# Single heads on quadrants of TensorE in an mLSTM followed by a rational feed-forward, with a work list derived anew

## The chip, the cores and the metric

One core of one Trainium2 chip runs the whole kernel. The metric is the device time of one execution, in microseconds; the kernel before takes 531.24 us, the median of three runs (530.92 to 532.42).

## What is computed

The reference has two stages. The first is a recurrent attention (mLSTM) over 4 batches of 8 heads, 768 steps, heads of 40 values:

```
for t in range(768):
    m_new = max(f[t] + m, i[t])
    fs, is_ = exp(f[t] + m - m_new), exp(i[t] - m_new)
    C = fs * C + is_ * outer(v[t], k[t])          # 40 x 40 per head
    n = fs * n + is_ * k[t]
    y[t] = sigmoid(o[t]) * (C @ q[t]) / max(abs(n . q[t]), 1)
```

The second takes the 3072 rows of 320 values through two matrices with a rational function between them:

```
h = x @ w_in                                      # 320 -> 2048
g = (a0 + a1 h + a2 h^2 + a3 h^3) / (1 + |b0||h| + |b1| h^2 + 1e-6)
out = g @ w_out                                   # 2048 -> 320
```

## The kernel before

**Attention.** The 768 steps are cut into chunks of 64 (`L`), and two chunks of one batch, 128 steps for all 8 heads, make a *unit*; there are 24 units, `u` = 0 to 23 (`attention`, line 841). Two units of neighbouring batches make a *pair*, `m` = 0 to 11 (`outputs`, line 1056). Heads go in twos: `NP` = 4 pairs of heads, the even head `j` = 0 on partitions 0 to 39 and the odd head `j` = 1 on partitions 64 to 103 of a tile of `DP` = 104 partitions. A unit's steps, each a piece of one engine's work, are: `lk`, `lq`, `lv`, `lf`, `la` (loads); `kp` (POOL scales the keys); `sc` (DVE's scan makes the decays `e`); `tk` and `ek` (PE transposes keys, ACT copies them to `kT`); `tq` and `eq` (PE transposes queries, ACT copies them to `qb`); `qa` (DVE, queries times decay, tile `qA`); `S` (PE, scores, tile `ps`); `P` (DVE, scores times decay, into tile `pm`); `ke` (POOL, decayed keys, the other part of `pm`); `ow` (PE, state products of the two chunks); `d0`, `u0`, `d1`, `u1` (POOL decays a state into `tm0` or `tm1`, DVE adds the product: states `sm` after the first chunk, `st` after the second). A pair's steps are `it` (PE, scores times values into two banks `y0` and `y1`), `i1` (PE adds queries times states to both banks), `ab`, `rc`, `g`, `x` (normalise and gate into `xn`), `xt`, `xh`, `xl` (transpose and split for the second stage, tile `xk`).

Two heads share one matmul by zeros in the operand: `qb` is cleared once in `_prologue` and `eq` writes the even head's queries into one half of its columns and the odd head's into the other half, with two copies of 40 partitions (lines 943 to 945). `S` (line 951) then makes 8 matmuls for a unit, each with 104 partitions, 64 columns of weights and 128 columns of queries. The states have the same form: `st` and `sm` hold 2 x 41 columns per pair of heads, with zeros where the two heads do not meet, so `decay` (line 987) works on 104 x 328 values, `update` (line 994) is two instructions of 40 partitions, and `inter` (line 1078) makes its matmuls with 104 partitions and 82 columns. Each bank `y{k}` holds heads 4k to 4k+3. `ow` reads only the decayed keys in `pm`, so it waits for `ke` and not for `P`. An f32 matmul stands in the trace as two instructions (two passes).

**Feed-forward.** Blocks of 256 rows (`n` = 0 to 11), eight tiles `i` of 256 of the 2048 columns each, make 96 tiles. A tile's steps are `f1` (PE, 16 single-pass matmuls of 256 columns, tile `ph`), `ha`, `p1`, `u`, `y`, `r0` (ACT), `p3`, `gh`, `m`, `gl` (DVE), `w`, `rm` (POOL), `f2` and `f3` (PE, 12 matmuls, tile `po`). The last tile of all is done in halves (names with `half`).

**Order.** Nothing is scheduled on the chip: `ORDER` (from line 145) is one written list of all steps, and `_Plan.listed` and `issue` emit them in that order, each engine following its own part of it strictly (`_Queue`). Six PSUM banks (`BANKS`, line 142) form one ring from which every `ph`, `ps`, `kq`, `ow`, `y` and `px` is taken; two hold `po`. Steps `hot` are 90 idle matmuls that fill PE during the start, `hz` another 24 at the end.

Of the kernel before, what the change touches and what calls it, by code (L numbers as in the profile page):

```python
# [141 lines left out]
BANKS = 6  # L142
# [15 lines left out]
sc_1 raw_i1 o0_o3 ogl_1 tq_1 raw_i2 eq_1 s1_j0 hot.65 gate.10 ow_0 pa_1 pc_1 pa_2 ke_1 o2_o3 zero.6 s0_o0.1 o2_o5
s3_j0 S_1 squares pc_2 qa_1 P_1 u0_0 ow_1 s2_o0 d1_0 hot.66 lk_3 raw_i5 lq_2 s1_o0.1 u0_1 hot.67 s0_o0 o0_j0 o2_j0
hot.68 hot.69 hot.70 hot.71 hot.72 hot.73 hot.74 hot.75 hot.76 s2_i1 s0_i1 u1_0 og_0 s3_o0.1 s1_o0 s1_i1 d1_1 raw_j1  # L160
s3_o0 it_0 i1_0 hot.77 hot.78 hot.79 ab_0 o0_o0 u1_1 s3_i1 pf_2 gate.11 sc_2 kp_2 tk_2 o2_j0.1 hot.80 s0_i2 it_0.1
rc_0 g_0 i1_0.1 ek_2 s2_i2 raw_o2 gate.12 s1_i2 ab_0.1 s0_i5 rc_0.1 gate.18 hot.81 x_0 hot.82 s3_i2 tq_2 hot.83
zero.9 ke_2 s1_i5 lv_2 hot.84 g_0.1 x_0.1 hot.85 gate zero.7 o0_i1 eq_2 hot.86 hot.87 pa_3 lq_3 oc_j0 raw_o4 lk_4
qa_2 o2_i1 s0_j1 s1_j1 xt_0 hot.88 xt_0.1 s2_i5 hot.89 pc_3 s3_i5 o2_o0 xh_0 s2_j1 o0_i2 xl_0 kp_3 s3_j1 ow_2 o0_i5
o2_i5 S_2 gate.1 tk_3 s0_o2.1 s0_o2 gate.13 u0_2 s1_o2 s2_o2 xh_0.1 s1_o2.1 d1_2 raw_o6 s3_o2 gate.14 raw_i7 u1_2
s3_o2.1 ek_3 xl_0.1 tq_3 o2_i2 o0_j1 s0_o4.1 eq_3 s0_o4 s2_o4 pf_3 P_2 f1_0_0 f1_0_0.1 o2_j1 gate.15 sc_3 gate.16
lv_3 lf_4 s1_o4.1 ke_3 kp_4 S_3 oc_j1 gate.19 s1_o4 s3_o4.1 s3_o4 ha_0_0 p1_0_0 s0_i7 f1_0_1 p3_0_0 P_3 u_0_0 lq_4
s1_i7 gate.17 o2_j1.1 s2_i7 o0_o4 ow_3 f1_0_1.1 s3_i7 w_0_0 s0_o6 o2_o4 y_0_0 ha_0_1 o0_i7 f1_0_2 f1_0_2.1 r0_0_0
lk_5 u0_3 gate.20 ogl_2 d1_3 qa_3 o2_i7 f1_0_3 gh_0_0 m_0_0 s1_o6 u_0_1 ha_0_2 w_0_1 p1_0_1 f2_0_0 f1_0_3.1 f2_0_0.1
# [6 lines left out]
u_0_5 m_0_4 o0_o6 rm_0_3 rm_0_4 ha_0_6 gl_0_3 qa_4 f3_0_3 xt_1.1 xh_1.1 w_0_5 f3_0_3.1 gate.25 gl_0_4 ow_4 S_4 u_0_6
p3_0_5 xl_1.1 zero.10 o2_o6 u0_4 P_4 p1_0_6 y_0_5 f2_0_4 r0_0_5 w_0_6 f1_1_0 d1_4 gh_0_5 m_0_5 f2_0_4.1 f3_0_4 tk_5
rm_0_5 ha_0_7 u_0_7 p3_0_6 w_0_7 ek_5 p1_0_7 u1_4 sc_5 f3_0_4.1 f1_1_0.1 y_0_6 ha_1_0 r0_0_6 gl_0_5 p3_0_7 gh_0_6
tq_5 f2_0_5 eq_5 f1_1_1 f1_1_1.1 f2_0_5.1 p1_1_0 qa_5 u_1_0 ke_5 d0_5 lk_6 gate.28 lq_6 lq_7 la_7 S_5 m_0_6 y_0_7
ha_1_1 r0_0_7 P_5 ow_5 f3_0_5 f3_0_5.1 p3_1_0 w_1_0 y_1_0 gh_0_7 m_0_7 f1_1_2 rm_0_6 rm_0_7 f2_0_6 ogl_8 gate.29  # L180
ogl_6 lf_6 gl_0_6 u_1_1 u0_5 w_1_1 f1_1_2.1 d1_5 p1_1_1 r0_1_0 gl_0_7 f2_0_6.1 f3_0_6 f3_0_6.1 f2_0_7 f2_0_7.1
gh_1_0 m_1_0 p3_1_1 f3_0_7 ha_1_2 p1_1_2 u1_5 p3_1_2 f3_0_7.1 it_2 i1_2 it_2.1 i1_2.1 lv_6 ev_0_7 u_1_2 ev_0_7.1
kp_6 y_1_1 ab_2 rc_2 sc_6 tk_6 rm_1_0 d0_6 g_2 r0_1_1 w_1_2 ke_6 f2_1_0 f2_1_0.1 lk_7 ab_2.1 ek_6 gh_1_1 gl_1_0
y_1_2 r0_1_2 x_2 m_1_1 rc_2.1 f1_1_3 f1_1_3.1 gate.26 tq_6 ha_1_3 p1_1_3 rm_1_1 gh_1_2 m_1_2 g_2.1 rm_1_2 f3_1_0
eq_6 gl_1_1 p3_1_3 u_1_3 f1_1_4 f1_1_4.1 ha_1_4 u_1_4 w_1_3 lv_7 x_2.1 qa_6 f3_1_0.1 f2_1_1 f2_1_1.1 gl_1_2 kp_7 S_6
ow_6 P_6 u0_6 p1_1_4 w_1_4 f3_1_1 p3_1_4 lf_7 lf_8 y_1_3 r0_1_3 f3_1_1.1 y_1_4 d1_6 gh_1_3 m_1_3 u1_6 f2_1_2 r0_1_4
xt_2 f1_1_5 f1_1_5.1 ha_1_5 f2_1_2.1 tk_7 ek_7 f3_1_2 f3_1_2.1 f2_1_3 f2_1_3.1 xh_2 u_1_5 d0_7 p1_1_5 xt_2.1 tq_7
gh_1_4 m_1_4 eq_7 xl_2 rm_1_3 gl_1_3 sc_7 p3_1_5 rm_1_4 ogl_7 w_1_5 ogl_12 gate.27 f1_1_6 f1_1_6.1 f1_1_7 xh_2.1
xl_2.1 f1_1_7.1 f3_1_3 f3_1_3.1 f1_2_0 f1_2_0.1 ha_1_6 p1_1_6 ke_7 p3_1_6 u_1_6 w_1_6 gl_1_4 y_1_5 qa_7 r0_1_5 ow_7
ogl_9 gate.30 lk_8 gh_1_5 m_1_5 rm_1_5 ha_1_7 S_7 u0_7 P_7 d1_7 gl_1_5 ha_2_0 y_1_6 f2_1_4 f2_1_4.1 f3_1_4 f3_1_4.1  # L190
f2_1_5 f2_1_5.1 u_1_7 it_3 lq_8 i1_3 la_8 it_3.1 i1_3.1 gate.31 ed_0_7 r0_1_6 p1_1_7 og_6 ab_3 la_9 ogl_10 ogl_11
u_2_0 kp_8 gh_1_6 u1_7 m_1_6 lq_9 sc_8 w_1_7 p3_1_7 rc_3 lv_8 rm_1_6 lf_9 p1_2_0 la_10 ed_0_7.1 g_3 w_2_0 tk_8 ek_8
# [135 lines left out]
def _prologue(ctx, tc, args):  # L328
# [50 lines left out]
def _program(  # L379
# [816 lines left out]
    def feed_forward(n, i):  # L1196
# [15 lines left out]
        def f_f1(j):  # L1212
            if j == 0:
                d["h"] = ring(psH, "h", [P, W], f"ph{n}_{i}")
# [216 lines left out]
```

## Time and profile before

| | us |
|---|---|
| median of three runs | 531.24 |
| lowest and highest | 530.92, 532.42 |
| span of the profiled execution | 527.5 |
| what the median has beyond that span | 3.7 |
| PE busy in the span | 499.9 |
| DVE, ACT, POOL busy | 449.0, 426.7, 382.8 |

The profile is of one execution. Its span runs from the first to the last instruction on the core. A busy PE is one that has a matmul in flight; how fast matmuls follow one another is read from the starts of consecutive groups in the timeline.

### The profile page before, as it was taken

To read this page: it belongs to the slowest core of one execution; us is meant where nothing else is said; L and a number is where in the kernel's file an instruction comes from. 1 tells how busy PE (TensorE), PEld (TensorE's weight loads), DVE (VectorE), ACT (ScalarE), POOL (GpSimd) and SP (SyncE) were. 2 spreads that over 40 slices of the span, in tenths; PEclk is the share of its full clock that TensorE was granted. 3 is DMA by queue.
4 is the path that set the end of the run, shared out by engine and by line. 5 is a ranking of instruction groups with operands and counts; after the bars stand their busy time and mean duration, and the time that the engine had idled before them with its cause. 6 is when DMAs were issued, how large, how long until landed. Compare 5 with 4: busy or idle time off the path is not lost.

```text
span 527.5 us, 12998 instructions
## 1 busy us (share of the span) xinstructions
PE 499.9 (95%) x4943; PEld 481.3 (91%) x4943; DVE 449.0 (85%) x798; ACT 426.7 (81%) x752; POOL 382.8 (73%) x360
## 2 busy tenths in 40 slices
PE   4889689999999999999999999999999999999993
PEld 4888579999999899999999999999999999999993
DVE  7999998999987998888887988889889888778770
ACT  2789899978889787787888988987787799888960
POOL 3668788998776877778676687777767767676760
PEclk8989999999999999999999999999999999999998
DMA  6978936246365320715700514302400410000001
GB/s 189 279 171 207 246 72 126 47 77 125 77 132 126 60 49 24 149 30 116 139 14 2 134 29 111 69 23 69 78 15 2 99 43 1 2 26 1 26 1 32
DMA packets 119113, 42.46 MB, mean 80 GB/s; under 512 B 103554, under 2 KB 111810, under 8 KB 119042
## 3 DMA queue, kind: packets, MB, share of 16 engines
q1 hardware_dynamic: 118912, 41.37, 35.7%
q8 instruction: 41, 0.67, 0.5%
q14 instruction: 30, 0.25, 0.2%
q10 hardware_dynamic: 130, 0.16, 0.1%
HBM read 36.90 MB, written 4.10 MB: 78 GB/s over the span
## 4 chain that ended last, share of the span: by engine, by line
PE 76%; DVE 9%; ACT 5%; issue 3%; POOL 2%; DMA 2%; SPq 2%; DVEq 0%; ACTq 0%
PE ph L34 30%; PE po L34 29%; PE y L34 4%; PE ps L34 4%; PE kq L34 3%; PE ow L34 2%; ACT ph L34 2%; SPq L34 2%; PE px L34 1%; DVE gH L34 1%; DVE gate_x L34 1%; DMA rawo<-in_moe_w_out_dram 1%; PE hot L34 1%; DMA qn<-in_q_dram 1%; DVE gL L34 1%
## 5 line engine op out<-in xcount | busy, mean ns | idle before, releaser
L34 POOL TENSOR_TENSOR p<-p,w 128x512 f32<-128x512 f32 (+1 forms) x97 | 129.2, 1332 | 81.1 <-DVE w L34 77.1
L34 PE MATMUL ph<-xk,wi 128*128 128x256 f32 x1152 | 170.5, 284 | 3.0 <-DVE xk L34 1.3
L34 PEld LDWEIGHTS ph<-xk,wi 128*128 128x128 f32 x1152 | 152.6, 188 | 4.8 <-DVE xk L34 1.7
L34 POOL TENSOR_TENSOR w<-w,ha 128x512 f32<-128x512 f32 (+1 forms) x97 | 129.5, 1338 | 13.1 <-ACT w L34 10.6
L34 PE MATMUL po<-wo,gH 128*128 128x320 f32 x768 | 137.4, 314 | 1.1 <-DVE gH L34 1.0
L34 PEld LDWEIGHTS po<-wo,gH 128*128 128x128 f32 x768 | 115.5, 188 | 3.5 <-DVE gH L34 1.9
L34 DVE SCALAR_TENSOR_TENSOR gH<-p,ps,ph 128x512 fp32r<-128x512 f32 (+1 forms) x97 | 71.4, 737 | 19.3 <-ACT ph L34 14.5
L34 DVE SCALAR_TENSOR_TENSOR gL<-p,ps,ph 128x512 fp32r<-128x512 f32 (+1 forms) x97 | 71.3, 736 | 17.7 <-POOL p L34 16.4
L34 ACT ACTIVATE ph<-w,cd 128x512 f32<-128x512 f32 (+1 forms) x97 | 66.4, 685 | 20.5 <-POOL w L34 11.3
L34 PE MATMUL po<-wo,gL 128*128 128x320 f32 x384 | 80.9, 318 | 1.8 <-DVE gL L34 1.8
L34 ACT ACTIVATE w<-ha,ba 128x512 f32<-128x512 f32 (+1 forms) x97 | 78.5, 811 | 3.9 <-POOL p L34 1.0
L34 DVE SCALAR_TENSOR_TENSOR w<-w,gH 128x512 f32<-128x512 f32 (+1 forms) x97 | 77.1, 794 | 4.4
L34 DVE SCALAR_TENSOR_TENSOR p<-p,ps,ph 128x512 f32<-128x512 f32 (+1 forms) x97 | 70.8, 735 | 6.1 <-ACT p L34 4.9
L34 ACT ACTIVATE ha<-ph 128x512 f32<-128x512 f32 (+1 forms) x97 | 57.2, 590 | 21.6 <-PE ph L34 21.0
L34 ACT ACTIVATE p<-ph,ps 128x512 f32<-128x512 f32 (+1 forms) x97 | 65.5, 676 | 3.1 <-DVE gL L34 3.0
L34 PEld LDWEIGHTS po<-wo,gL 128*128 128x128 f32 x384 | 59.1, 188 | 4.1 <-DVE gL L34 2.5
L34 ACT ACTIVATE ph<-ph 128x512 f32<-128x512 f32 (+1 forms) x97 | 56.2, 580 | 2.2
L34 PE MATMUL ph<-xk,wj 128*128 128x256 f32 x192 | 54.2, 282 | 0.0
L34 PE MATMUL ph<-xk,wY 128*128 128x256 f32 x192 | 54.1, 282 | 0.0
L34 PEld LDWEIGHTS ph<-xk,wj 128*128 128x128 f32 x192 | 36.2, 189 | 0.0
L34 PEld LDWEIGHTS ph<-xk,wY 128*128 128x128 f32 x192 | 36.2, 189 | 0.0
L34 PE MATMUL hot<-ident 128*128 128x128 f32 x180 | 26.1, 301 | 4.0 <-DVE flag_out L374 4.0
(133 smaller groups left out, 749.0 us busy)
## 6 DMA issues: line engine op xcount, KB each, us to landing
rawo<-in_moe_w_out_dram SPq DMA_DIRECT2D x8, 640.0 KB
ab<-scrA SPq DMA_DIRECT2D x40, 128.0 KB
rawi<-in_moe_w_in_dram SPq DMA_DIRECT2D x8, 512.0 KB
kr<-in_k_dram SPq DMA_DIRECT2D x24, 160.0 KB
qn<-in_q_dram SPq DMA_DIRECT2D x24, 160.0 KB
vb<-in_v_dram SPq DMA_DIRECT2D x48, 80.0 KB
og<-in_o_gate_dram SPq DMA_DIRECT2D x48, 80.0 KB
out_dram<-ot SPq DMA_DIRECT2D x23, 160.0 KB
```

What stands on the lines that cost most here:

```text
L34: made = fn(*args, **kwargs)
```

## The change

1. **Scores.** `qb` with its zeros goes; `eq` is one copy of 104 partitions into a tile `qT`. `S` makes 16 matmuls per unit in place of 8, each for one head: 40 partitions (0 to 39 or 64 to 103), 64 columns of weights, 64 columns of queries, consecutive ones on the four combinations of upper or lower partitions and upper or lower output. Even heads go to bank `ps0`, odd heads to `ps1`, so a unit's scores take two of the six banks. `P` becomes two steps, one per bank.
2. **States.** `st` and `sm` lose their zeros: 41 columns per pair of heads in place of 82. `decay` works on 104 x 164 values, `update` is one instruction of 104 partitions in place of two of 40, and eight memsets at the start go, as does that of `qb`. `ow` has 64 columns of weights in place of 40, so that all 104 rows of its output are written; the two parts of `pm` change places, and the 24 extra columns are the first ones of the scores, so `ow` now waits for both steps `P`.
3. **Banks by parity.** `y{k}` holds the heads of parity k. `i1` is one step in place of two, after both `it`: for each state, 4 pairs of heads, 2 units and 2 parities it makes a matmul of 40 partitions, 64 columns of weights and 41 columns of state: 32 for a pair where there were 16. `g` and `x` address every second head.
4. **Rest.** The gates `o` are loaded and put through the sigmoid in six groups of four units in place of seven. The two halves of the very last tile get a bank each.
5. **List.** `ORDER` is another list throughout (2769 steps for 2766).

The core of the diff, without the list:

```diff
@@ f_eq, f_S, f_P @@
-            nc.scalar.copy(qb[0:D, :, :, 0], pq()[0:D])
-            nc.scalar.copy(qb[L:DP, :, :, 1], pq()[L:DP])
+            nc.scalar.copy(qT.rearrange("p n c t -> p (n c t)"), d["kq"][0:DP])
...
-            ps = d["ps"] = bank("ps")
+            d["ps"] = [ring(psH, "h", [P, 512], f"ps{j}_{u}", at=plan.many["h"][j]) for j in range(2)]
             for p in range(NP):
                 for c in range(2):
-                    nc.tensor.matmul(
-                        ps[c * L : (c + 1) * L, p * 2 * L : (p + 1) * 2 * L],
-                        d["kT"][:, p, c * L : (c + 1) * L],
-                        qb[:, p, c].rearrange("p j t -> p (j t)"),
...
+                    for j in range(2):
+                        r = slice(j * L, j * L + D)
+                        nc.tensor.matmul(
+                            d["ps"][j][c * L : (c + 1) * L, p * L : (p + 1) * L],
+                            d["kT"][r, p, c * L : (c + 1) * L],
+                            qT[r, p, c],
...
-                d["pm"][:, :, 0:L], d["ps"].rearrange("p (h t) -> p h t", h=H), d["e"], ALU.mult
+                d["pm"][:, j::2, D:DP], d["ps"][j][:, 0 : NP * L].rearrange("p (h t) -> p h t", h=NP),
+                d["e"][:, j::2], ALU.mult,
@@ f_ow, decay, update @@
-                    ow[j * L : j * L + D, p * 2 * E1 : (p + 1) * 2 * E1],
-                    d["pm"][:, h, L:DP],
+                    ow[j * L : (j + 1) * L, p * 2 * E1 : (p + 1) * 2 * E1],
+                    d["pm"][:, h, 0:L],
...
-            d[c] = ap1.tile([DP, NP, 2 * E1], F32, tag=f"tm{c}", name=f"tm{u}_{c}")
+            d[c] = ap1.tile([DP, NP, E1], F32, tag=f"tm{c}", name=f"tm{u}_{c}")
...
-            for j in range(2):
-                r = slice(j * L, j * L + D)
-                own = d["ow"][r, 0 : NP * 2 * E1].rearrange("p (n c e) -> p n c e", n=NP, c=2)[:, :, c]
...
+            own = d["ow"][0:DP, 0 : NP * 2 * E1].rearrange("p (n c e) -> p n c e", n=NP, c=2)[:, :, c]
+            if n + c == 0:
+                nc.vector.tensor_copy(dst, own)
+            else:
+                nc.vector.tensor_tensor(dst, d[c], own, ALU.add)
@@ the plan of a unit @@
-        add("P", "DVE", 0.60, f_P, r=["ps", "e"], w=["pm.0"])
+        for j in range(2):
+            add("P", "DVE", 0.45, lambda j=j: f_P(j), r=[f"ps{j}", "e"], w=[f"pm.0{j}"])
...
-        add("ow", "PE", 0.85, f_ow, r=["pm.1", V], w=["ow"], new=new("ow"))
+        add("ow", "PE", 0.85, f_ow, r=["pm.1", "pm.00", "pm.01", V], w=["ow"], new=new("ow"))
@@ inter @@
-        def inter(k):
-            for i in range(2):
-                for x in range(len(pair[0]["states"])):
+        def inter():
+            for x in range(len(pair[0]["states"])):
+                for p in range(NP):
                     for j in range(2):
                         c, state = pair[j]["states"][x]
-                        p = 2 * k + i
-                        nc.tensor.matmul(
-                            ye(k)[j * L : (j + 1) * L, 2 * i : 2 * i + 2, c],
-                            pair[j]["qA"][:, p, c], state[:, p].rearrange("p j e -> p (j e)"),
-                            start=False, stop=True, skip_group_check=True,
-                        )
+                        for k in range(2):
+                            r = slice(k * L, k * L + D)
+                            nc.tensor.matmul(
+                                ye(k)[j * L : (j + 1) * L, p, c], pair[j]["qA"][r, p, c], state[r, p],
+                                start=False, stop=True, skip_group_check=True,
+                            )
```

In the new list the end of a pair reads, for pair 8 and in most others alike: `ow_17 u0_17 ... it_8 it_8.1 i1_8`. In the list before it read `... it_8 it_8.1 ... i1_8 i1_8.1`, with `u0_17` a good deal earlier.

## Rows read from the trace of the kernel before

**Rows 1.** The page's first lines: the span, and each engine's busy time (share of the span) and instructions.
```profile
span 527.5 us, 12998 instructions
PE 499.9 (95%) x4943; PEld 481.3 (91%) x4943; DVE 449.0 (85%) x798; ACT 426.7 (81%) x752; POOL 382.8 (73%) x360
```

**Rows 2.** The busy time of each engine in stretches of the span (us from its start), with instructions, granted clock, share of the DMA engines and GB/s.
```profile
core 0: us, PE busy (x) PEld busy (x) DVE busy (x) ACT busy (x) POOL busy (x), PEclk, DMA share, GB/s
0.00:20.00 20.00, 13.12 (x110) 12.75 (x111) 16.54 (x49) 9.04 (x16) 8.82 (x24) 0.91 0.77 234
20.00:45.00 25.00, 21.97 (x317) 20.30 (x315) 24.46 (x52) 20.44 (x36) 18.93 (x20) 0.93 0.92 205
45.00:70.00 25.00, 20.06 (x279) 17.83 (x279) 24.01 (x53) 22.92 (x45) 19.26 (x20) 1.00 0.86 198
70.00:95.00 25.00, 22.60 (x223) 21.25 (x221) 22.21 (x42) 24.37 (x44) 20.46 (x19) 1.00 0.48 90
95.00:145.00 50.00, 50.00 (x532) 48.34 (x529) 47.42 (x81) 41.75 (x75) 42.18 (x38) 1.00 0.44 86
195.00:245.00 50.00, 50.00 (x523) 47.70 (x523) 43.06 (x74) 38.56 (x69) 38.80 (x35) 1.00 0.32 68
395.00:445.00 50.00, 50.00 (x468) 48.87 (x467) 42.14 (x70) 43.16 (x75) 36.40 (x32) 1.00 0.16 38
515.00:527.50 12.50, 4.35 (x37) 4.16 (x36) 0.65 (x2) 0.53 (x1) 0.00 (x0) 0.80 0.11 33
```

**Rows 3.** What PE waited for, all of it over 0.4 us: us in total, times, longest.
```profile
PE hot L34 <- DVE flag_out L374: 4.0, 1, 4.0
PE pe L34 <- DVE gate_m L34: 2.9, 1, 2.9
PE pa L34 <- DVE zo L34: 2.3, 1, 2.3
PE kq L34 <- DVE zo L34: 2.1, 2, 1.5
PE po L34 <- DVE gL L34: 1.8, 2, 0.9
...
PE po L34 <- DVE gH L34: 1.0, 2, 0.6
```

**Rows 4.** The timeline of PE between 200 and 240 us: start, us from the first start to the last end, and the instructions merged; form as partitions * columns of weights, then partitions x columns streamed.
```profile
203.58 0.28 PE L34 MATMUL ph<-xk,wY 128*128 128x256 f32 x1
203.79 0.79 PE L34 MATMUL y<-vb,pm 128*64 128x82 f32 x16
204.42 0.31 PE L34 MATMUL y<-st,qA 104*64 104x82 f32 x4
204.56 0.31 PE L34 MATMUL y<-sm,qA 104*64 104x82 f32 x4
...
204.99 0.74 PE L34 MATMUL y<-vb,pm 128*64 128x82 f32 x16
205.56 0.31 PE L34 MATMUL y<-st,qA 104*64 104x82 f32 x4
...
206.23 1.44 PE L34 MATMUL po<-wo,gH 128*128 128x320 f32 x8
...
209.41 0.75 PE L34 MATMUL po<-wo,gL 128*128 128x320 f32 x4
210.00 0.75 PE L34 MATMUL po<-wo,gH 128*128 128x320 f32 x4
...
215.26 0.75 PE L34 MATMUL po<-wo,gL 128*128 128x320 f32 x4
215.93 1.10 PE L34 MATMUL ps<-qb,kT 104*64 104x128 f32 x16
216.96 0.55 PE L34 MATMUL px<-ident,xn 128*128 128x128 f32 x3
...
226.00 0.77 PE L34 MATMUL ow<-vb,pm 128*40 128x82 f32 x16
226.70 0.85 PE L34 MATMUL po<-wo,gH 128*128 128x320 f32 x4
```

**Rows 5.** The timeline of PE from 516 us: a run of f32 passes over the full array.
```profile
515.85 3.51 PE L34 MATMUL hz<-ident 128*128 128x128 f32 x30
```

**Rows 6.** The timeline of PE from 36.8 us: a run of passes of 64 columns, on the upper and the lower 64 outputs in turn.
```profile
36.76 2.03 PE L34 MATMUL pa<-g,ident 128*64 128x64 f32 x64
```

**Rows 7.** The instructions of tile `ps` from 93 us to the end, and of tile `y` from 110 us to the end: duration in ns (least, median, most), first and last start.
```profile
L34 PE MATMUL ps<-qb,kT x320: 270/273/324, 94.1 to 455.0; 104*64 104x128 f32 x160
L34 PE MATMUL y<-vb,pm x320: 232/233/286, 110.7 to 462.0; 128*64 128x82 f32 x160
L34 PE MATMUL y<-st,qA x160: 232/234/237, 111.4 to 462.5; 104*64 104x82 f32 x160
L34 PE MATMUL y<-sm,qA x160: 232/234/234, 111.5 to 462.6; 104*64 104x82 f32 x160
```

**Rows 8.** The weight loads of tiles `ps` and `ow` over the span, in the same columns.
```profile
L34 PEld LDWEIGHTS ps<-qb,kT x384: 132/137/230, 28.8 to 454.8; 104*64 104x64 f32 x192
L34 PEld LDWEIGHTS ow<-vb,pm x384: 112/117/118, 36.2 to 455.5; 128*40 128x40 f32 x192
```

**Rows 9.** Groups of one line and form: busy us, mean ns of one, then the idle time of the engine before them and its releaser.
```profile
L34 ACT COPY qb<-kq 40x512 f32<-40x512 f32 x48 | 27.8, 579 | 2.1 <-PE kq L34 1.7
L34 ACT ACT_TABLE_LOAD x15 | 19.2, 1283 | 4.8 <-DVE flag_out L374 3.8 <-DVE p L34 0.7
L34 POOL TENSOR_TENSOR tm<-sm,ab 104x328 f32<-104x328 f32 x24 | 17.9, 747 | 2.6 <-DVE sm L34 2.3
L34 DVE TENSOR_TENSOR pm<-ps,e 128x512 f32<-128x512 f32 x24 | 16.5, 687 | 2.2 <-PE ps L34 1.9
L34 DVE TENSOR_TENSOR sm<-tm,ow 40x164 f32<-40x164 f32 x40 | 12.8, 319 | 1.7 <-PE ow L34 1.0
L34 DVE TENSOR_TENSOR xk<-px,xk 128x256 fp32r<-128x256 f32 x24 | 10.1, 420 | 2.3 <-ACT xk L34 2.2
L34 DVE SCALAR_TENSOR_TENSOR w<-w,gH 128x512 f32<-128x512 f32 x95 | 76.1, 801 | 4.4
```

**Rows 10.** The chain that ended last, between 55 and 70 us: start, us, what.
```profile
59.98 5.08 DMA qn<-in_q_dram
```

More of the change, by code (lines that the diff above doesn't have):

```diff
@@ L176 @@
[L176 to L180, printed above, removed]
@@ L439, in _program @@
     qn = [common["qn0"], cp.tile([P, H, L], F32, name="qn1")]
-    kp, qb = common["kp"], common["qb"]
+    kp = common["kp"]
+    qT = cp.tile([DP, NP, 2, L], F32, name="qT")
     vb = [common["vb0"], cp.tile([P, H, 2, E1], F32, name="vb1")]
-    st = [cp.tile([DP, NP, 2, E1], F32, name=f"st{j}") for j in range(B + 2)]
-    sm = [cp.tile([DP, NP, 2, E1], F32, name=f"sm{j}") for j in range(2)]
+    st = [cp.tile([DP, NP, E1], F32, name=f"st{j}") for j in range(B + 2)]
+    sm = [cp.tile([DP, NP, E1], F32, name=f"sm{j}") for j in range(2)]
     wt = {}
@@ L716, in setup @@
         plan.add("zero", "DVE", 0.25, lambda: ones(nc.vector, vb[0]), w=["vb0"])
-        later = [("qn1", qn[1], 0.5), ("vb1", vb[1], 0.8), *((f"sm{j}", t, 0.3) for j, t in enumerate(sm))]
-        later += [(f"st{j}", t, 0.3) for j, t in enumerate(st)]
-        for name, t, cost in later:
-            names = [f"{name}.0", f"{name}.1"] if name[0] == "s" else [name]
-            plan.add("zero", "POOL", cost, lambda t=t: clear(nc.gpsimd, t), w=names)
+        for name, t, cost in (("qn1", qn[1], 0.5), ("vb1", vb[1], 0.8)):
+            plan.add("zero", "POOL", cost, lambda t=t: clear(nc.gpsimd, t), w=[name])
         plan.add(
@@ L1142, in outputs @@
         for k in range(2):
-            y = f"y{k}.{m}"
             y = f"y{k}at{m}"
-            add("it", "PE", 0.6, lambda k=k: f_it(k), r=[*(f"pm_{u}.0" for u in us), "vb0", "vb1"], w=[y],
+            add("it", "PE", 0.6, lambda k=k: f_it(k), r=[*(f"pm_{u}.0{k}" for u in us), "vb0", "vb1"], w=[y],
                 new=[(y, home(f"y{k}"))])
-        for k in range(2):
-            add("i1", "PE", 0.6, lambda k=k: inter(k), r=[x for j in pair for x in j["i1"]], w=[f"y{k}at{m}"])
+        add("i1", "PE", 0.6, inter, r=[x for j in pair for x in j["i1"]], w=[f"y{k}at{m}" for k in range(2)])
         for k in range(2):
@@ L1210, in chunk, with hh @@
             return i if size == 2 else 2 * i + j
+        def hh(c):
+            return d["h", c.start // T][:, 0 : c.stop - c.start] if last else d["h", 0][:, c]
         def f_f1(j):
-            if j == 0:
-                d["h"] = ring(psH, "h", [P, W], f"ph{n}_{i}")
+            if j == 0 or last:
+                d["h", j] = ring(psH, "h", [P, W], f"ph{n}_{i}_{j}")
             c = chunk(j)
@@ L1324, in own @@
                     return x
-                return f"{x}{k}" if part is None or not last else f"{x}{k}.{part}"
+                if part is None or not last:
+                    return f"{x}{k}"
+                return f"h{k}p{part}" if x == "h" else f"{x}{k}.{part}"
             plan.add(
@@ L1329, in add @@
                 [own(x) for x in r], [*(own(x) for x in w), f"turn {name}"],
-                [(f"{x}{k}" if x in BUFS or x == "h" else x, t) for x, t in new], **kw,
+                [(own(x).split(".")[0], t) for x, t in new], **kw,
             )
@@ L1343, in feed_forward @@
             f = chunk(j)
-            add("f1", "PE", 0.9, lambda j=j: f_f1(j), w=["h"], new=[("h", ("h", BANKS))] if j == 0 else (), part=j,
+            add("f1", "PE", 0.9, lambda j=j: f_f1(j), w=["h"], new=[("h", ("h", BANKS))] if j == 0 or last else (), part=j,
                 r=[*xs, f"wi{f // 2}", f"wi{f // 2}.l",
@@ L1391, in _program @@
     for u in range(NU):
[L1392 to L1393 removed]
+        if u % 4 == 0:
+            gates_o(u, 4)
         attention(u)
```

387 lines of the change are left out of this document (190 added, 197 removed).

## The prediction

> **What bounds the kernel now.** I first read the page's head: span 527.5 us, PE busy 95% of it, DVE 85%, ACT 81%, POOL 73% [rows 1]. Such shares are means over unlike stages, so the second view is busy time by stretch [rows 2]. There are three stages. Up to 95 us PE is busy 77.8 of 95 us while DVE is busy 48.5 of the 50 us from 20 to 70, with the DMA engines at 0.86 to 0.92: the start is set by DVE and the loads, and PE is padded there with idle matmuls. From 95 to 515 us PE is busy all of its time (50.00 of 50.00 in three of the stretches shown), DVE 42 to 47 of 50. The last 12.5 us are drain. The third view confirms it: all that PE ever waits for in the middle is under 3 us on `gH` and `gL`; the other waits belong to the start [rows 3]. So after 95 us a microsecond taken out of PE's own queue is a microsecond of the kernel, as long as the other engines keep up, and before 95 us PE's time is worth nothing and DVE's is worth something.
>
> Since a busy PE only means a matmul in flight, I price PE by starts in its timeline. A run of full-array f32 passes of 128 columns: (3.51 - 0.27) / 29 = 0.11 us a pass [rows 5, 7]. `S` has 16 passes of 128 columns in 215.93 to 216.96, hardly more than 8 x 0.11 = 0.88 [rows 4]: two passes, on the upper and the lower half of the outputs, take the time of one. So before already has two tiles of the array side by side, by columns. `it` and `i1`, 82 columns: 0.57 for 16 passes, 0.071 a pair [rows 4]. `pa`, 64 columns, with the same 64-column weights as `S`: (2.03 - 0.23) / 31 = 0.058 a pair [rows 6, 7]. What the trace does not have is a matmul on half the partitions: all take 104 or 128.
>
> **The change, part by part.**
>
> *Scores.* 16 passes in 8 pairs become 32 in 8 groups of four (upper or lower partitions, upper or lower outputs), of 64 columns. If the four run side by side, a group costs what a pair of 64 columns costs, 0.058: 8 x 0.058 = 0.46 for 0.88, 0.42 saved. From 95 us on there are 19 units (20 starting at 94.1 us, less the first [rows 7]): 8.0 us. The bounds for a group are 0.058 and two pairs, 0.116. I take the low end: columns already give full overlap here, and rows are read from other partitions and written to another bank.
>
> *States times queries.* For a pair `m`, 32 passes of 82 columns (16 pairs, 16 x 0.071 = 1.14) become 64 passes of 41 columns in 16 groups. The stream shrinks: the line through 0.110 at 128 columns and 0.058 at 64 gives 0.039 at 41. The weights don't: still 64 columns. A load of 64 columns takes 137 ns and one of 40 takes 117 [rows 8], 0.83 ns a column, so 64 are 0.053 of loading, about the 0.058 at which `pa` runs. I take 0.058 (bounds 0.039 and 0.116): 16 x 0.058 = 0.93, 0.21 saved. Ten pairs come after 95 us [rows 7]: 2.1 us.
>
> *Changes of the array's form.* The trace shows a price for going from full-array work to half-column work and back: four `po` passes ahead of `S` take 0.67 against 0.59 ahead of more `po`, and `S` has 1.03 - 0.88 = 0.15 at its end; `ow` has 0.70 - 0.57 = 0.13, a pair's `it` and `i1` 2.44 - 4 x 0.57 = 0.16 [rows 4]. That is about 0.23 for an island, 0.12 a change. Counted in the two lists from `f1_1_0` on, PE changes form 68 times before and, if quarter work (`S`, `i1`) and half work (`ow`, `it`) count as two forms, 87 times after: between `it` and `i1`, and where `S` and `ow` stood together. 19 x 0.12 = 2.3 us lost. If quarter against half costs nothing, only four changes are new, 0.5 us. I take 2.3, since the nearest row is a change with a stall. The Trainium skill (TensorEngine Tiling (Array Packing), Key Properties) says that a change of tiling mode drains the engine, and also that different tiles load weights and multiply in parallel; by that page the sum is the same as mine, and no row of before shows tiles split by rows.
>
> *A tighter end of each pair.* The list now has `ow`, `u0`, `it`, `it.1`, `i1`. `i1` waits for `u0`, which waits for `ow`; between `ow` and `i1` PE has only the two `it`, 1.14 us. `ow`'s last pass is 0.23 in flight [rows 7], `u0` takes 0.32 [rows 9]: some 0.5 of slack, and on DVE one instruction of up to 0.80 (`m` [rows 9]) may stand ahead. So most pairs pass, some wait 0.3 or more, and behind `i1` on PE is the feed-forward, the bound. I take 1.0 us over ten pairs; bounds 0 and 5.0 (0.5 each).
>
> *DVE, ACT, POOL.* DVE: `u0` and `u1` are four instructions of 0.32 a unit, then two; `P` is one of 0.69, then two of about 0.42 (the row of 128 x 256 values): -0.64 + 0.15 = -0.49 a unit [rows 9]. ACT: one copy of 0.58 fewer a unit, and two table loads of 1.28 fewer with six sigmoid groups for seven. POOL: the decays of 0.75 become about half, and nine memsets go. After 95 us all this lies beside PE and counts nothing; it does keep the cover: in 95 to 145 us DVE is at 47.4 of 50 [rows 2], and four to five units there give back 2.2, about as much as PE shortens. Should PE stop being the bound there, the 0.49 is the gain left.
>
> *Start.* Four to five units fall before 95 us: 5 x 0.49 = 2.4 off DVE, which is the bound along with the loads. The list is new, though; its first `f1` comes after 17 of the 18 weight loads, against 18, and after about the same DVE work, so no more than part of that arrives. I take 1.0 gained; bounds 2.0 gained and 5.1 lost, the length of one load on which the chain of before ran [rows 10].
>
> *Priced at nothing.* `ow` waits for `P`: by the list and the durations above, all but two or three units have over a microsecond of other PE work between; without it, one wait of about a microsecond. Scores in two of six banks: PE never waits for a bank now [rows 3]; without that slack `f1` would wait for one ACT or DVE step, 0.8. Wider weights in `ow`: 0.053 of loading under 0.071 of streaming. Banks of their own for the last two halves: in the drain, at most 0.5.
>
> *Sum.* 8.0 + 2.1 - 2.3 - 1.0 + 1.0 = 7.8 us. The profiled span goes from 527.5 to 519.7; the median lies 3.7 above that span, so 531.2 becomes **523.4**.
>
> **The rivals.** *No four at once (slower).* Either halves by partitions don't run beside each other, or PE can't be fed more densely than the densest stretch in the trace, `pa` with 0.029 a pass [rows 6]. Both give 0.116 a group. `S`: 0.93 for 0.88, 1.0 lost over 19 units; `i1`: 1.86 for 1.14, 7.2 lost over ten pairs; with 2.3, 1.0 and +1.0 as above 10.5 us lost: 541.7. It decides from 0.083 a group on: there 152 x (0.110 - g) + 160 x (0.071 - g) equals the 2.3 of the changes of form. For it: no row below 0.058 a pair, and PE's instructions for `S` and `i1` double. Against it: the halves by columns overlap almost perfectly. The Trainium skill (TensorE: Matmul & The Clock Gate, "Wait — 56ns, not 53.3ns?") has a rule against this change: start to start never drops below about 25 ns, however small the matmul. By that rule, as an estimate, `S` takes 0.80 and `i1` 1.60 and the kernel 536.6; the trace has starts 0.029 apart on the mean, so it doesn't decide.
>
> *Given back in waits (no change).* The four run at once, but `i1` waits 0.5 in each pair (5.0), and the new start reaches the feed-forward some 3 us later: 10.1 - 2.3 - 5.0 - 3.0, about nothing: 531.4. For it: the tight pairs, and a start with the loads at 0.9. Against it: DVE has less to do per unit everywhere.
>
> **How the numbers follow.** The forecast's case gets 0.68. Its own range: at best 8.0 + 10 x (1.14 - 0.62) - 0.5 + 2.0 = 14.7 saved, 516.5; at worst, with part of the waits, 530. The no-four rival gets 0.20, the given-back rival 0.12, of which 0.02 over the bound. Differences of 0.3% (1.6 us) are about what a measurement of this kernel can tell from none. So faster 0.68, same 0.10, slower 0.22. The range takes in the forecast's case and the given-back rival and leaves out the no-four rival: 516.5 to 533.
>
> **What would show it.** In the timeline after, the 32 passes of `S` should take 0.6 from their start to PE's next work (1.03 before), and `i1` about 1.0 for its 64; groups of four should start within a few hundredths. If `S` takes over 0.9 and `i1` 1.9, the rival is right. Between `it.1` and `i1` there should be 0.1 and now and then a wait on DVE `sm`; waits there of 0.5 every time would be the second rival. PE should be full from about 95 us on. The prediction is wrong at its root if PE shows waits on DVE or ACT after 95 us that it does not show now.

## The result, and the profile after

The changed kernel takes 516.37 us (median of four runs, 515.76 to 516.95) against 531.08 us (529.25 to 532.42) for the kernel before in the same runs: a ratio of 0.9715 (95% interval 0.9688 to 0.9741), 14.7 us less. The forecast was 7.8 us less, 523.4, and its range ended at 516.5: the direction and the saving on PE came out, but the gain is nearly twice as large and the time lies just outside the range. The profiled execution took 516.0 us with a span of 513.8.

The page's head of the changed kernel, as [rows 1]:

```profile
span 513.8 us, 14398 instructions
PE 493.2 (96%) x5679; PEld 476.2 (93%) x5679; DVE 432.8 (84%) x774; ACT 408.1 (79%) x726; POOL 368.0 (72%) x351
```

All four engines are busy for less time. PE's busy time falls by 6.7 us only, since a matmul in flight counts the same whether one or four share the array; the matmuls have to be read by their starts. The timeline of PE around a unit's `S` (start, us, merged instructions, form), as [rows 4]:

```profile
206.58 0.75 PE L34 MATMUL po<-wo,gL 128*128 128x320 f32 x4
207.26 0.69 PE L34 MATMUL ps<-qT,kT 40*64 40x64 f32 x32
207.88 0.55 PE L34 MATMUL px<-ident,xn 128*128 128x128 f32 x3
```

From the start of `S` to PE's next work it is 207.88 - 207.26 = 0.62 us, 1.03 before [rows 4], though twice as many passes run. In the single records the four passes of a group start 6 to 7 ns apart and groups follow every 58 ns. The same view around the end of a pair:

```profile
193.68 0.79 PE L34 MATMUL y<-vb,pm 128*64 128x82 f32 x16
194.30 0.74 PE L34 MATMUL ow<-vb,pm 128*64 128x82 f32 x16
...
197.34 0.79 PE L34 MATMUL y<-vb,pm 128*64 128x82 f32 x16
198.06 0.68 PE L34 MATMUL y<-st,qA 40*64 40x41 f32 x32
198.55 0.66 PE L34 MATMUL y<-sm,qA 40*64 40x41 f32 x32
199.13 0.57 PE L34 MATMUL po<-wo,gL 128*128 128x320 f32 x2
```

An `it` followed by work of its own form takes 0.62 (193.68 to 194.30), and one followed by the quarter-array `i1` takes 0.72 (197.34 to 198.06): the change between half and quarter work costs 0.10 us. `i1` takes 199.13 - 198.06 = 1.07. No wait on DVE's `sm` stands ahead of it, here or in any other pair. What PE waited for in all (us in total, times, longest), as [rows 3]:

```profile
PE hot L34 <- DVE flag_out L370: 4.0, 1, 4.0
PE ps L34 <- ACT lo0o L34: 2.5, 1, 2.5
PE pe L34 <- DVE g L34: 2.4, 1, 2.4
PE ow L34 <- POOL p L34: 1.3, 1, 1.3
...
PE po L34 <- DVE gL L34: 0.4, 1, 0.4
```

The long waits belong to the start. Busy time by stretch, as [rows 2]:

```profile
core 0: us, PE busy (x) PEld busy (x) DVE busy (x) ACT busy (x) POOL busy (x), PEclk, DMA share, GB/s
...
70.00:95.00 25.00, 25.00 (x280) 24.31 (x278) 24.30 (x48) 22.34 (x43) 21.74 (x19) 1.00 0.45 77
95.00:145.00 50.00, 50.00 (x689) 47.71 (x687) 46.10 (x79) 41.12 (x72) 41.13 (x40) 1.00 0.52 106
```

PE is full from 70 us on but for one wait of 0.7 at 169 us (`kq` on ACT's `kT`); between 70 and 95 it was at 22.60 of 25 before, and DVE has 46.1 us of work in 95 to 145 where it had 47.4.

**Where the 13.8 us of span went.** The last matmul of the feed-forward's first layer (`ph`) and what follows it, in the timeline of PE at the end, first of the kernel before:

```profile
504.88 0.29 PE L34 MATMUL ph<-xk,wY 128*128 128x256 f32 x1
...
513.39 0.85 PE L34 MATMUL po<-wo,gL 128*128 128x320 f32 x4 [0.92 <-DVE gL L34]
```

where the closing run of idle matmuls starts at 515.85 [rows 5], and of the kernel after:

```profile
494.27 0.28 PE L34 MATMUL ph<-xk,wY 128*128 128x256 f32 x1
494.39 0.61 PE L34 MATMUL hz<-ident 128*128 128x128 f32 x4
...
497.21 0.85 PE L34 MATMUL po<-wo,gL 128*128 128x320 f32 x4 [0.44 <-DVE gL L34]
...
501.92 5.07 PE L34 MATMUL hz<-ident 128*128 128x128 f32 x44
```

Three parts add up. To the first `ph` matmul: 59.23 us after 60.00, 0.8 gained. From the first to the last: 494.27 - 59.23 = 435.04 after 504.88 - 60.00 = 444.88, 9.8 gained. From the last to the closing run of idle matmuls: 501.92 - 494.27 = 7.65 after 515.85 - 504.88 = 10.97, 3.3 gained (0.1 is lost behind it).

The second and third part are not cut at the same work, though. The passes of `po` behind the last `ph` (count in brackets), before and after:

```profile
504.88:527.54 22.66, 8.79 (x52) 0.89 0.06 20
494.27:513.75 19.48, 6.80 (x40) 0.93 0.07 23
```

The new list puts 12 more of them ahead of the last `ph`, 12 x 0.147 = 1.8 us of PE's time (four take 0.59 [rows 4]). With the same work on both sides the stretch from first to last gained 11.6 and the end 1.5.

Summed from start to start over PE's records, with PE's idle time left out, `S` takes 7.3 us less (21 units) and `i1` 1.9 less, `it` and `ow` 0.5 more each: together -8.2. PE's idle time between the first and the last `ph` falls from 5.1 to 2.0, and 2.5 of these 3.1 stand before 95 us. Seven idle matmuls that the new list has behind the first `f1` add 1.6, the 12 passes of `po` 1.8. The remaining 1.9 are gained in passes of the feed-forward and the transposes that follow one another a little closer; why is not shown.

The median adds another 0.9: the runs lie 3.5 us above the span before (531.08 - 527.54) and 2.6 after (516.37 - 513.75). The profiled execution before was a quick one, since the other executions of that kernel have spans of 527.4 to 531.9.

### The profile page after: what moved, and what is told of

It is laid out like the page before. It is cut to its first block, busy times and chain, and to the rows that moved or that the text cites. A ratio compares the mean times of both kernels' runs of the same rounds, so it can differ in the third digit from the quotient of the medians.

```text
span 513.8 us, 14398 instructions
## 1 busy us (share of the span) xinstructions
PE 493.2 (96%) x5679; PEld 476.2 (93%) x5679; DVE 432.8 (84%) x774; ACT 408.1 (79%) x726; POOL 368.0 (72%) x351
## 4 chain that ended last, share of the span: by engine, by line
PE 77%; DVE 7%; ACT 5%; DMA 3%; SPq 2%; POOL 2%; issue 2%; DVEq 0%; ACTq 0%; POOLq 0%
PE ph L34 31%; PE po L34 30%; PE y L34 4%; PE kq L34 3%; PE ow L34 3%; SPq L34 2%; PE ps L34 2%; ACT ph L34 2%; POOL p L34 2%; PE px L34 1%; DMA kr<-in_k_dram 1%; DVE w L34 1%; PE hz L34 1%; DVE gH L34 1%; DMA rawo<-in_moe_w_out_dram 1%
## 5 line engine op out<-in xcount | busy, mean ns | idle before, releaser
L34 POOL TENSOR_TENSOR w<-w,ha 128x512 f32<-128x512 f32 (+1 forms) x97 | 127.6, 1319 | 24.2 <-ACT w L34 22.4
L34 PE MATMUL po<-wo,gH 128*128 128x320 f32 x768 | 135.2, 313 | 0.0
L34 DVE SCALAR_TENSOR_TENSOR w<-w,gH 128x512 f32<-128x512 f32 (+1 forms) x97 | 80.0, 825 | 3.5
L34 DVE SCALAR_TENSOR_TENSOR gL<-p,ps,ph 128x512 fp32r<-128x512 f32 (+1 forms) x97 | 71.3, 736 | 13.8 <-POOL p L34 12.9
L34 PE MATMUL po<-wo,gL 128*128 128x320 f32 x384 | 79.6, 317 | 0.5 <-DVE gL L34 0.4
L34 PE MATMUL hot<-ident 128*128 128x128 f32 x180 | 30.0, 323 | 4.0 <-DVE flag_out L370 4.0
```

The costliest lines, as they stand in the source:

```text
L34: made = fn(*args, **kwargs)
```

## Experiments

Each kernel is the changed one with the edit shown, except where it says otherwise; times are medians with their lowest and highest run, beside the kernel before at 531.3 to 532.2 in the same jobs. From job to job that kernel moves by up to 1.1, so differences of less than about 1 us decide nothing.

**Are upper and lower partitions really side by side?** In `f_S` the loop over the two halves of the partitions goes outside, so that all passes on the upper ones are queued ahead of all on the lower ones:

```diff
-            for p in range(NP):
-                for c in range(2):
-                    for j in range(2):
+            for j in range(2):
+                for p in range(NP):
+                    for c in range(2):
```

> The changed kernel, with one loop turned round in S: all 16 passes on the upper partitions first, then all 16 on the lower, so that only the two halves by columns can run side by side. Theory A (the four quarters run at once, and PE is the bound, so its time counts one for one): a unit's S goes from 0.62 to 1.08 us (16 x 0.058 for 8 x 0.058), 20 units after the start, 9.3 us more than the 516.4 of the changed kernel: 525.7. Theory B (the gain is the new list and the lighter vector engines, PE has room): within 2 us of 516.4, whatever S takes. If S stays at 0.62, quarters by rows were never what made it shorter.

Measured: 522.21 us (521.68 to 522.65), 5.8 more than the changed kernel. Its timeline of PE:

```profile
210.55 0.98 PE L34 MATMUL ps<-qT,kT 40*64 40x64 f32 x32
211.45 0.55 PE L34 MATMUL px<-ident,xn 128*128 128x128 f32 x3
```

`S` takes 0.90 where it took 0.62, not the 1.08 expected. The single records name no partitions, but they fall into two rhythms: a second row of pairs begins 0.295 us after the first pass, when 10 of the first row's 16 have started, and from there both rows run on, a pair every 58 ns each. Read as the two halves, each keeps a pace of its own, and PE began work that is queued behind unstarted work of the other half; the full gain needs them interleaved. The same for `i1`, with `for k in range(2)` put outside the loops over `p` and `j`:

> The changed kernel, with the loop over the parity k put outside in i1, so that passes on the upper partitions all come before those on the lower, for each state. Theory A: 32 pairs of 0.058 for 16 groups of 0.058, 0.93 us more for each of ten pairs of units: 525.7. Theory B: within 2 us of 516.4.

Measured: 519.81 us (518.91 to 519.97), 3.4 more. Here the records name the tiles, since all passes on `sm` are queued behind all on `st`:

```profile
198.68 0.76 PE L34 MATMUL y<-st,qA 40*64 40x41 f32 x26
199.22 0.25 PE L34 MATMUL y<-sm,qA 40*64 40x41 f32 x2
199.26 0.23 PE L34 MATMUL y<-st,qA 40*64 40x41 f32 x2
```

The first passes on `sm` start while six on `st` are still to come. In both kernels what PE loses is what the kernel loses: `S` takes 0.28 longer in 21 units, 5.9 for 5.8, and `i1` 3.4 longer in all for 3.4. PE is the bound. Both losses are below the 9.3 expected, since the halves still overlap in part.

**What sets the pace of `i1`?** Its 41 columns of stream should take less than 58 ns; its weights have 64 columns. With 48:

```diff
-                                ye(k)[j * L : (j + 1) * L, p, c], pair[j]["qA"][r, p, c], state[r, p],
+                                ye(k)[j * L : j * L + 48, p, c], pair[j]["qA"][r, p, c, 0:48], state[r, p],
```

> The changed kernel, but i1 loads 48 of the 64 weight columns and so leaves the state part of the last 16 steps of each chunk out of the result. What a group of four costs in i1 is 58 ns by the starts, as in S, though it streams 41 columns and S 64. If loading the weights sets it: 48 columns take (48/64) x 53 = 40 ns and some 5, a group about 45 ns, and the kernel 10 x 16 x 0.013 = 2.1 us less: 514.3. If the feeding of instructions sets it (eight in 58 ns), or the columns streamed, nothing changes: 516.4.

Measured: 514.39 us (514.35 to 514.74), 2.0 less. Its timeline of PE:

```profile
197.20 0.79 PE L34 MATMUL y<-vb,pm 128*64 128x82 f32 x16
197.92 0.57 PE L34 MATMUL y<-st,qA 40*48 40x41 f32 x32
198.30 0.55 PE L34 MATMUL y<-sm,qA 40*48 40x41 f32 x32
```

Eight groups take 0.38 from start to start where 64 columns take 198.55 - 198.06 = 0.49; in the single records a group takes 45 ns for 58. Neither the stream nor the feeding of instructions, both unchanged, can be what bound `i1`. It goes with the columns of weights: 13 ns for 16 columns, 0.81 a column, where the loads differ by 0.83 a column [rows 8]. That fits the loading, as the forecast put it; the outputs written shrink along with the weights, and no run separates the two. (This kernel leaves out part of the result.)

**The end.** Both halves of the very last tile go back into one bank:

```diff
-            return d["h", c.start // T][:, 0 : c.stop - c.start] if last else d["h", 0][:, c]
+            return d["h", 0][:, c]
```

> The changed kernel with both halves of the very last tile in one PSUM bank, as before (the list still keeps the second bank free). If the banks of their own make the end shorter (1.5 us of the gain lie behind the last f1, by PE's gaps there): 517.3 to 518. If the end is shorter by the order of the list alone: 516.4 within 0.5.

Measured: 519.37 us (519.07 to 520.2), 3.0 more. The timeline of ACT in this kernel (in brackets the idle time before and its releaser):

```profile
491.75 0.58 ACT L34 ACTIVATE ph<-ph 128x512 f32<-128x512 f32 x1
494.47 0.38 ACT L34 ACTIVATE ha<-ph 128x256 f32<-128x256 f32 x1 [2.14 <-PE ph L34]
...
495.45 0.67 ACT L34 ACTIVATE ph<-w,cd 128x512 f32<-128x512 f32 x1
```

and of the changed kernel:

```profile
491.87 0.58 ACT L34 ACTIVATE ph<-ph 128x512 f32<-128x512 f32 x1
492.38 0.37 ACT L34 ACTIVATE ha<-ph 128x256 f32<-128x256 f32 x1
...
493.42 0.69 ACT L34 ACTIVATE ph<-w,cd 128x512 f32<-128x512 f32 x1
```

With one bank ACT's reading of the first half waits 2.14 us for PE's writing of the second. Behind it in ACT's queue stands `y` of the tile ahead (the 512-wide `ph<-w,cd`), 2.0 us later for it, so DVE's `gH` and then PE's `po` are late. PE's own timeline of the kernel with one bank:

```profile
499.23 0.86 PE L34 MATMUL po<-wo,gL 128*128 128x320 f32 x4 [2.57 <-DVE gL L34]
499.92 2.03 PE L34 MATMUL po<-wo,gH 128*128 128x320 f32 x8
```

The wait of 2.57 is followed by eight passes that take 2.03 for the usual 1.33: the granted clock is 0.57 of full speed from 500 to 502 us, most of that time on the lower of its two levels (1.2 of 2.4 GHz), where it is 1.00 in the changed kernel. With the new list, one bank costs a wait and then a slow stretch.

With the list of before it costs less. In the kernel before, ACT's reading of the first half waits for PE's last `ph` too, but only 0.43 us:

```profile
505.20 0.39 ACT L34 ACTIVATE ha<-ph 128x256 f32<-128x256 f32 x1 [0.43 <-PE ph L34]
```

From the last `ph` to the end of the span it is 22.7 us in the kernel before (old list, one bank), 21.7 with the old list and two banks (the last run below), 23.0 with the new list and one bank (this run) and 19.5 with both new. So neither the second bank nor the new list makes the end short by itself.

**Were the late idle matmuls in the way?** The changed list has seven `hot` matmuls after the first `f1`; here they stand ahead of it:

```diff
-u0_2 f1_0_0 f1_0_0.1 hot.83 hot.84 S_3 ha_0_0
+u0_2 hot.83 hot.84 hot.85 hot.86 hot.87 hot.88 hot.89 f1_0_0 f1_0_0.1 S_3 ha_0_0
```

> The changed kernel with the seven idle matmuls that the new list has behind the first f1 put in front of it. They take 1.6 us of PE between 59 and 67 us. If PE waits there for something else anyway: 516.4 within 0.5. If they stand in the way: 514.8 to 515.8.

Measured: 516.9 us (516.69 to 517.81), 0.5 more and inside the spread: they don't stand in the way.

**Is the relief of the vector engines worth anything?** First all three engines' work is done twice: the copy `eq` on ACT, the decays on POOL, the updates on DVE.

```diff
+            for _ in range(2):
                 nc.scalar.copy(qT.rearrange("p n c t -> p (n c t)"), d["kq"][0:DP])
...
+            for _ in range(2):
                 nc.gpsimd.tensor_tensor(
...
+            for _ in range(2):
                 if n + c == 0:
```

> The changed kernel with the work that the change took from the vector engines put back as idle repeats: the copy eq, each decay and each state update are made twice, with the same result (per unit 0.59 us on ACT, 0.65 on DVE, 0.8 on POOL). If PE alone is the bound and the fewer waits come from the list: 516.4 to 518.4 (only the start and the tight ends of pairs feel it). If the fewer waits come from the lighter engines: 520 to 523, with new waits of PE on DVE sm between it and i1.

Measured: 531.97 us (531.12 to 533.21), 15.6 more, beyond both expectations: the whole gain is gone. Then one engine at a time, first DVE:

> The changed kernel with each state update on DVE made twice (0.65 us a unit, as many instructions as before the change), the rest as changed. All three repeats together cost 15.6 us. Theory D (DVE is the second bound: 46.1 of 50 us busy from 95 to 145 us, 42 to 43.6 later): most of it, 8 to 13 us, 525 to 529. Theory L (it is the latency of the steps u0 and d1, which the tight ends of pairs feel, on whatever engine): 4 to 6, 520 to 522, about the same as with the decays.

ACT:

> The changed kernel with the copy eq on ACT made twice (0.59 us a unit). Theory D: ACT is busy 79%, and S comes microseconds behind eq in PE's order: 516.4 to 518.5. Theory L: S waits for it where it stands close behind (units 4 to 9), 518 to 520.

and POOL:

> The changed kernel with each decay on POOL made twice (0.4 us each, as long as before the change). Theory D: POOL is busy 72% and d0, d1 are not in the tight ends: 516.4 to 518.5. Theory L: 520 to 522.

Measured: 516.67 with DVE's work twice, 516.74 with ACT's, 526.4 (525.45 to 527.01) with POOL's. DVE or ACT alone cost 0.3 and 0.4, within the spread, so neither theory named the engine. But POOL's doubling is no return to the work before: the groups of the changed kernel by line and form (busy us, mean ns, idle time before) are

```profile
L34 POOL TENSOR_TENSOR tm<-sm,ab 104x164 f32<-104x164 f32 x24 | 14.9, 620 | 5.5 <-DVE sm L34 5.5
L34 POOL TENSOR_TENSOR tm<-st,ab 104x164 f32<-104x164 f32 x20 | 11.2, 559 | 0.0
```

so half the values take 620 ns for 747 before [rows 9], and twice 620 is far more than 747. The nearer test makes the decays work on 328 values again, of which half are used:

```diff
+            wide = ap1.tile([DP, NP, 2, E1], F32, tag=f"tm{c}", name=f"tm{u}_{c}")
             nc.gpsimd.tensor_tensor(
-                d[c], src, d["ab"][0:DP, c, :, L - 1 : L].broadcast_to([DP, NP, E1]), op=ALU.mult,
+                wide, src.unsqueeze(2).broadcast_to([DP, NP, 2, E1]),
+                d["ab"][0:DP, c, :, L - 1 : L].unsqueeze(2).broadcast_to([DP, NP, 2, E1]), op=ALU.mult,
             )
+            d[c] = wide[:, :, 0]
```

> The changed kernel with each decay on POOL writing 104 x 328 values again (the narrow state read twice), so 0.75 in place of 0.58 us as before the change; pool_twice put back three times as much as the change had taken (2 x 0.58 for 0.58). Theory P (POOL's time counts in proportion, 10 us for 24 x 1.1 us): the true relief of about 0.36 us a unit is worth 3 to 4 us, 519.4 to 520.4. Theory Q (the list has room for some tenths and not for a microsecond): 516.4 to 517.5, and the shorter decays were not where the unforeseen gain came from.

Measured: 518.43 us (517.92 to 519.13), 2.1 more. Its decays take 897 and 836 ns for 747 and 784 before, so it still overshoots:

```profile
L34 POOL TENSOR_TENSOR tm<-sm,ab 104x328 f32<-104x328 f32 x24 | 21.5, 897 | 4.4 <-DVE sm L34 4.3
```

Last, this together with `eq` and the updates twice: quadrants on PE, and about the vector work of before (somewhat more, since `P` stays two steps and the decays take 905 and 860 ns).

> The changed kernel with all the vector work of the state and query steps as long as before the change: eq twice, updates twice, decays 104 x 328 (the memsets and table loads stay away). Theory P: 520 to 521. Theory Q: 516.4 to 518, and the step of the prediction that priced the vector engines' relief at nothing after 95 us holds.

Measured: 523.08 us (521.51 to 524.18), 6.7 more than the changed kernel and more than either theory had, though the three parts alone cost 0.3, 0.4 and 2.1. Busy time by stretch in this kernel:

```profile
95.00:145.00 50.00, 47.60 (x624) 44.98 (x623) 45.74 (x81) 39.11 (x69) 39.64 (x36) 0.97 0.46 97
```

and the wait in its timeline of PE:

```profile
136.28 0.56 PE L34 MATMUL po<-wo,gL 128*128 128x320 f32 x2
138.66 0.67 PE L34 MATMUL kq<-ident,kp 128*104 128x128 f32 x2 [1.81 <-DVE gL L34]
```

PE is no longer full between 95 and 145 us: it waits 1.81 for DVE's `gL`, and from 139 to 143 us the granted clock is 0.62. From 95 us to the last `ph` PE is idle for 3.6 us, 0.7 in the changed kernel. By the first matmul of each block of 256 rows the kernel is 0.8 us behind the changed one at block 0, 1.3 at block 1, 6.0 at block 2 (148.44 for 142.47) and 7.5 at the end. So most of it is lost in the stretch in which DVE is fullest, and the price there is a wait and then the clock, as with one bank at the end. The clock does not fall behind every such wait: in the kernel before with the new list (below) PE waits 1.88 at 143 us and 2.56 at 515 us, and the clock stays at 1.00 behind both.

The other way round, one engine is loaded with another's work, the decays on DVE in place of POOL (`nc.vector` for `nc.gpsimd`):

> The changed kernel with both decays on DVE (about 0.33 us each) in place of POOL (0.58). DVE bore 0.65 us a unit more at no cost, POOL did not bear 1.1 us more. Theory P: less work on POOL takes waits away, of which PE has some 3 us left after the first f1: 514.5 to 516. Theory Q: 516.4 within 0.6; if DVE can't bear steps that sit ahead of its own chain, 517 to 519.

Measured: 522.0 us (521.96 to 523.14), 5.6 more, outside all three ranges. DVE needs 691 and 636 ns for what POOL does in 620 and 559, twice what was expected. That DVE has no room for these 1.3 us a unit is likely, not shown: it took 0.65 a unit at no cost when the updates were made twice.

**List and arithmetic.** The kernel before gets the changed kernel's list, with its own steps in it (`P_u` for the two steps `P`, `i1_m i1_m.1` for `i1_m`, the eight memsets back) and the gates in six groups:

```diff
-        if u % 4 == 2 or u == 0:
-            gates_o(u, 2 if u in (0, NU - 2) else 4)
+        if u % 4 == 0:
+            gates_o(u, 4)
```

> The kernel before (zeros, half-array S and i1, one bank of scores, six more memsets and a copy more per unit) in the order of the new list, with the sigmoid groups of four that this list needs; P and i1 stand where the new list has them. Theory A (8.0 us of the 14.7 are PE's own work, the rest is the list): 516.4 + 8.0 = 524.4, 522 to 526. Theory B (the list is nearly all of it): below 520. Theory C (the list is only good with the new durations, and its tight ends of pairs wait with the old ones): 528 or more.

Measured: 534.36 us (534.14 to 536.5), 3 more than the kernel before, as theory C had it. Its first `f1` comes at 63.1 us for 60.0, as much as the kernel loses; between the first and the last `ph` PE is idle for 3.5 us there (0.9 before 95 us) for 5.1 (3.8). And the changed kernel with the list of before (`P_u P_u.1` for `P_u`, one `i1_m`, the gates in seven groups, steps that would otherwise be out of order put later, the `ow` of nine units among them):

> The changed kernel in the order of the list before: the two steps P where P stood, i1 where its second half stood, sigmoid groups as before, and 21 steps (ow of nine units above all, which now wait for P) a few places later where their inputs or a bank are not there yet. Theory A: 531.1 - 8.0 = 523.1, 521 to 525. Theory B: 528 or more.

Measured: 562.47 us (561.93 to 562.67), 46 more than the changed kernel. Its waits of PE begin

```profile
PE ow L34 <- issue: 10.1, 7, 4.6
```

The profile names no releaser for these waits of `ow`; by the program, where the old list has `S` directly ahead of `ow`, `ow` now waits for `P`, which waits for `S`. From the first to the last `ph` PE is idle for 24.1 us, 12.9 of them ahead of `ow`. Neither list serves the other arithmetic, so these two runs don't split the gain between them: the new list alone gains nothing, and the new arithmetic needs it.

## Why the prediction was right in sign and wrong in size

Three things were sized wrong: 3.4 us of shorter waits and closer passes (less the idle matmuls) that had no term, the end, which gained 1.4 and stood at nothing, and 1.0 set aside for the pairs. The rest is small.

**PE's own terms held.** Scores, states times queries and changes of form were to save 8.0 + 2.1 - 2.3 = 7.8 us over 19 units; over the 21 units after the first `ph` that is 7.8 x 21 / 19 = 8.6, and 8.2 was measured. A group of four takes the 58 ns that it was given, `i1` 1.07 for "about 1.0", and a change between half and quarter work 0.10 for the 0.12 that was priced from the island of before. That quarter work counts as a form of its own was the right choice of the two.

**No four at once: refuted.** `S` takes 0.62 and not 0.93, and queueing the halves apart costs 5.8 and 3.4 us. The rule of the Trainium skill (TensorE: Matmul & The Clock Gate, "Wait — 56ns, not 53.3ns?"), which spoke for this rival with its floor of about 25 ns from start to start, doesn't hold here for passes on different quadrants: four passes in 58 ns are 14.5 ns each on the mean, 6 to 7 ns inside a group, and the measurement decides.

**A tighter end of each pair (1.0 us): not paid.** `i1` found `u0` done in every pair. The waits that were feared did not come, so "given back in waits" falls too.

**The start (1.0 us): 0.8 at the first `f1`, and 2.5 behind it that had no term.** The forecast gave DVE's relief as the reason. The runs bear that out in part: the first `f1` comes at 60.35 with the updates on DVE twice, at 59.98 with the copy on ACT twice and at 59.99 with about the vector work of before, for 59.23 (59.1 to 59.2 in three kernels that leave the start alone, 60.00 before). So the 0.8 hangs on the relief, but on ACT's as well as on DVE's. Behind the first `f1` and before 95 us PE's idle time fell from 3.8 to 1.3. It stays as low with about the vector work of before (1.0) and in the kernel before with the new list (0.9), so this part is the list's; the forecast had taken the list as a risk and given it no gain. The seven idle matmuls fill 1.6 of it.

**The end: the step that failed.** "Banks of their own for the last two halves: in the drain, at most 0.5" put nothing into the sum. With one bank the kernel takes 3.0 us more, 519.4, which would have been inside the range. The 0.5 is about the wait of the kernel before (0.43), and in the old list a second bank shortens the end by 1.0. What the forecast did not ask is what the new list makes of it: there 12 more passes of `po` stand ahead of the last `ph`, and behind the waiting `ha` in ACT's queue stands the tile ahead, which DVE and then PE's `po` are waiting for. With the same work on both sides the end gained 1.5 us over the kernel before, which is the size that this term should have had.

**"After 95 us all this lies beside PE and counts nothing": wrong as a price, not what made the sum short.** Taken away, the relief costs 6.7 us: with quadrants but vector work about as before, the kernel takes 523.1. But the forecast let PE's saving through in full, saying of the relief that "it does keep the cover", and did the sum for 95 to 145 us (DVE 47.4 of 50, relief 2.2, PE's saving about the same). The run shows that the cover was needed, as the forecast had said. From 95 us on PE is idle for 0.7 where it was idle for 1.3 before, so beyond that the relief added little that shows as idle time. That 523.1 is nearly the forecast's 523.4 is no confirmation, since that kernel has the 3 us of the end, which the forecast had not; without them it would come out at about 526, an estimate by adding the two runs. How much of the 6.7 is overshoot of the wide decays and of the two steps `P` is open; by itself POOL's part is 2.1.

**The sum after the fact.** To the 7.8 come 0.4 for the two earlier units, 1.0 that the pairs did not cost, 3.1 of waits and 1.9 of closer passes less 1.6 for the idle matmuls, and 1.5 less 0.1 for the end; 0.2 is missing at the start. That makes 13.8 of span. The 0.9 that the median now lies closer to its span makes 14.7, as measured. The lower bound of 516.5 allowed for a cheaper `i1`, which did not come, and left out the end and the waits, which did: that it was missed by only 0.1 us is luck.

What stays open is what the 1.9 us of closer passes come from.

## What to carry to other kernels

Small matmuls on 40 of 64 partitions and 64 columns run four at a time if the four quadrants are interleaved in the queue; price a group by the columns of its weights and count each change of form (0.10 us here). When the bound engine gets shorter, the relief of the others is not free slack: here 6.7 of 14.7 us hung on it. Work out stretch by stretch whether they can follow; in two of these runs a wait in PE's full stream was followed by the lower clock as well. And in a drain, look for engines that share a bank or a tile in halves, and price the sharing in the new order of the steps, not in the old: a wait there holds up all that is queued behind it.

## What was not expected of the hardware

- PE starts passes on one half of the partitions ahead of earlier queued ones on the other: with the halves of `i1` queued apart, passes on `sm` start at 199.22 us while six on `st`, queued ahead of them, are still to come.
- The parts of the vector relief don't add: 0.3, 0.4 and 2.1 us alone, 6.7 together.
- POOL's time follows the size of its work only in part: 104 x 164 values take 620 ns where 104 x 328 took 747 [rows 9], and 104 x 328 with the state repeated by a broadcast take 897.
